# Attention decode: P times V summed in four PSUM quadrants instead of one row

## The chip, the cores and the metric

The kernel runs on one core of a Trainium2 chip. The metric is the device time of one execution in microseconds, the median over the runs. A profile of one execution is taken beside the times; its span runs from the first to the last instruction on the core, and some time of the execution lies outside of it.

## The reference

One query row for each of 16 heads attends to 8192 keys of width 256; everything is bfloat16.

```
B, H, Sq, Sk, D = 1, 16, 1, 8192, 256
scale = q.shape[-1] ** -0.5
scores = jnp.einsum("bhqd,bhkd->bhqk", q, k) * scale
p = softmax(scores, axis=-1)
return jnp.einsum("bhqk,bhkd->bhqd", p, v)
```

K and V are 67 MB each and every element is used once.

## The kernel before, in words

**Tiles.** A head's K (and V) is one SBUF buffer of 128 partitions by 64 x 256: partition p holds the keys 64p to 64p + 63, and "column j" means the 128 keys 64p + j, a block of 128 x 256. There are two K buffers and two V buffers, used by even and odd heads.

**Scores.** VectorE makes the scores of columns 0 to 47 (`head`, line 191: multiply a block by the query, which stands in every partition, and sum along the row). TensorE makes those of columns 48 to 63: it transposes the blocks (`ktrans`, line 280), ScalarE copies the transposes to SBUF (`evac`, line 376), and matmuls with the query give 16 columns of scores (`kscore`, line 294), which ScalarE copies (`scopy`, line 380) next to VectorE's.

**Softmax.** VectorE reduces the 64 scores of each partition to a maximum (line 207). A matmul lays these 128 maxima into one row of the PSUM tile `mx` (`transpose_m`, line 228, columns 0 to 127), VectorE takes their maximum (`xmax`, line 173), a matmul with ones spreads it over the partitions (`bcast`, line 234), and ScalarE computes the exponentials E and their sum per partition (`expo`, lines 384 and 388). A matmul with ones adds the sums (`total`, line 244), VectorE takes the reciprocal (`recips`, line 178).

**P times V.** `pv` (line 259) runs 64 matmuls: the stationary operand is one column of E (128 x 1), the moving one a block of V (128 x 256), and all 64 are summed in row 0 of the PSUM tile `acc` of the head's parity. ScalarE scales that row by the reciprocal (`final`, line 401) and issues the output's DMA (line 408).

**Order.** Each engine has its own queue, written out by hand; semaphores join them. A loop turn handles two heads. TensorE in turn i: scores of the even head 2i; `pv` of head 2i-2, with `transpose_m`, `bcast` and `total` of head 2i-1 placed behind its columns 32, 48 and 64; scores of the odd head 2i+1; `pv` of head 2i-1; `total` of head 2i. ScalarE in turn i: the four copies, `scopy` and the next query for each of the two heads, the exponentials where they come due, and at the end of the turn `final` of heads 2i-2 and 2i-1. VectorE: the even head, then the odd head; the reciprocals of the two heads before stand behind column 2 of each. After the loop the exponentials and the two finals of heads 14 and 15 follow.

**Loads.** SyncE issues all K and V loads in one order (line 136): K of head h+2, then V of head h. K of head h+2 waits until VectorE has finished head h (`kd`), V of head h until `pv` of head h-2 is done. A load is 4096 KB; the V of heads 14 and 15 comes in pieces, that of head 15 in nine, the last two of two columns each, so that `pv` can follow the data closely. The semaphores that stand for "the round before" are given their first values by GpSimd (`AHEAD`), behind its memsets at the start.

Of the kernel before, what the change touches and what calls it, by code (L numbers as in the profile page):

```python
# [6 lines left out]
ACT = mybir.ActivationFunctionType  # L7
AX = mybir.AxisListType
FP32 = mybir.dt.float32
# [4 lines left out]
K_FIRST = (16, 32)  # L14
V_HALVED = 13
V_LATE = {14: (0, 16, 32, 48), 15: (0, 16, 28, 38, 46, 52, 57, 60, 62)}
AHEAD = {"kd": 1, "sc": 1, "sp": 2, "ex": 2, "m": 1, "g": 1, "mT": 1, "l": 2, "bc": 1, "nb": 1, "rc": 2, "pv": 2, "fin": 4}
V_SEMS = (("va0", "v0b", "v0c", "v0d"), ("va1", "v1b", "v1c", "v1d", "v1e", "v1f", "v1g", "v1i", "v1j"))


class _Step:
# [19 lines left out]
def bass_standalone__mha_softmax__decode_kernel(nc: bass.Bass, q: bass.AP, k: bass.AP, v: bass.AP, out: bass.AP):  # L41
    B, H, Sq, D = q.shape
    Sk = k.shape[2]
    P = 128
    J = Sk // P
# [26 lines left out]
    with contextlib.ExitStack() as ctx:  # L72

        def sb(name, shape, d):
            return ctx.enter_context(nc.sbuf_tensor(name, shape, d))
# [19 lines left out]
        m = sb("m", [P, 2], FP32)  # L95
        g = sb("g", [1, 2], FP32)
# [4 lines left out]
        identb = sb("identb", [P, P], BF16)  # L101
        ones_row = sb("ones_row", [1, P], FP32)
        ones_col = sb("ones_col", [P, 1], FP32)
        o_sb = [sb(f"o_sb{i}", [1, D], out.dtype) for i in range(2)]

        acc = [ps(f"acc{i}", [P, 512]) for i in range(2)]
        tp = [ps(f"tp{i}", [P, GRP * D], BF16) for i in range(2)]
        spe = ps("spe", [P, 512])
        mx = ps("mx", [P, 512])
# [2 lines left out]

        for name in ("qc", "pool", "cb", "cf", "qp", "qs", "qb", "kd", "tp", "kt", "sp", "sc", "m", "mT", "g", "bc", "nb", "ex"):
            sem(name)
        for name in ("l", "rc", "pv", "fin", "ldq", "k0", "k0a", "k0b", "k1", "va0", "va1", "v1h", "o0", "o1"):
            sem(name)
        late = [name for row in V_SEMS for name in row[1:] if name not in ("v0c", "v1c")] + ["v1h"]
        for row in V_SEMS:
# [6 lines left out]
        if True:  # L125
# [15 lines left out]
            @(lambda f: f(nc.gpsimd))  # L141
            def _(pool):
                def step(ins, n):
                    ins.then_inc(sem("pool"), 1)
                    pool.wait_ge(sem("pool"), n)

                def eye(t, n, done):
                    step(pool.memset(t[:, :], 0.0), n)
                    pool.affine_select(
                        out=t[:, :],  # L150
                        in_=t[:, :],
                        compare_op=ALU.not_equal,
                        fill=1.0,
                        base=0,
                        pattern=[[-1, P]],
                        channel_multiplier=1,
                    ).then_inc(sem(done), 1)

                eye(identb, 1, "cb")
                eye(ident, 2, "cf")  # L160
                pool.memset(ones_row[:, :], 1.0).then_inc(sem("cf"), 1)
                pool.memset(ones_col[:, :], 1.0).then_inc(sem("cf"), 1)
                pool.memset(q_all[:, H * QW : (H + 1) * QW], 0.0).then_inc(sem("cf"), 1)
                for name, n in AHEAD.items():
                    pool.nop().then_inc(sem(name), n)
                for name in late + ["o0", "o1", "va0", "va1"]:
                    pool.nop().then_inc(sem(name), 32 if name in ("o0", "o1") else 16)
# [57 lines left out]
            def _(pe):  # L225
# [16 lines left out]
                def total(h):  # L242
# [6 lines left out]
                        stop=True,  # L249
                    ).then_inc(sem("l"), 1)  # L250

                def pv(h, waits, at):

                    pe.wait_ge(sem("fin"), h.of(1, 3))
                    pe.wait_ge(sem(f"va{h.par}"), h.of(8, 32 - 8 * h.par))
                    for j in range(J):
                        for name, value in waits.get(j, ()):
                            pe.wait_ge(sem(name), value)
                        ins = pe.matmul(  # L259
                            acc[h.par][0:1, 0:D],  # L260
                            lhsT=E[h.par][:, j : j + 1],
                            rhs=vbuf[h.par][:, j * D : (j + 1) * D],
                            start=(j == 0),
                            stop=(j == J - 1),
                        )
                        if j == J - 1:
                            ins.then_inc(sem("pv"), 1)
                        if j + 1 in at:
                            at[j + 1]()
# [33 lines left out]
                def scores(t, before=None):  # L303
# [15 lines left out]
                    rhs=q_sb[:, :],  # L319
# [26 lines left out]
                with pe.Fori(0, H // 2 + 1) as i:  # L346
                    ev, od = _Step(0, i), _Step(1, i)
                    fin_turn = pe.snap((i // 8) * 16 + 16)
                    half_turn = pe.snap(((i + 1) // 8) * 16 + 16)
                    old = od.back(2)  # L350
                    with pe.If(i < H // 2):
                        scores(ev)
                    with pe.If(i > 0):
                        pv(
                            ev.back(2),
                            {V_LATE[14][n]: [(V_SEMS[0][n], fin_turn)] for n in range(1, len(V_SEMS[0]))},
                            {32: lambda: transpose_m(old), 48: lambda: bcast(old), 64: lambda: total(old)},
                        )
                    with pe.If(i < H // 2):
                        scores(od, before=ev)  # L360
                    with pe.If(i > 0):
                        waits = {V_LATE[15][n]: [(V_SEMS[1][n], fin_turn)] for n in range(1, len(V_SEMS[1]))}
                        waits[HALF] = [("v1h", half_turn)]
                        pv(old, waits, {})
                    with pe.If(i < H // 2):
                        total(ev)

            @(lambda f: f(nc.scalar))
            def _(act):
# [12 lines left out]
                def expo(h):  # L382
                    act.wait_ge(sem("bc"), h.of(1, 2))
                    act.activation(  # L384
                        out=negb[:, h.par : h.par + 1], in_=sm[:, 0:1], func=ACT.Copy, scale=-1.0
                    ).then_inc(sem("nb"), 1)
                    act.wait_ge(sem("nb"), h.of(1, 2))
                    act.activation(  # L388
                        out=E[h.par][:, :],
                        in_=S[h.par][:, :],  # L390
                        func=ACT.Exp,
                        bias=negb[:, h.par : h.par + 1],
                        scale=1.0,
                        accum_out=lsum[:, h.par : h.par + 1],
                    ).then_inc(sem("ex"), 1)

                def final(h, dst):
                    act.wait_ge(sem("rc"), h.of(1, 3))
                    act.wait_ge(sem("pv"), h.of(1, 3))
                    act.wait_ge(sem(f"o{h.par}"), h.of(8, 32 - 8 * h.par))  # L400
                    act.activation(  # L401
                        out=o_sb[h.par][0:1, :],
                        in_=acc[h.par][0:1, 0:D],
                        func=ACT.Copy,
                        scale=recip[0:1, h.par : h.par + 1],
                    ).then_inc(sem("fin"), 1)
                    act.wait_ge(sem("fin"), h.of(1, 5))
                    act.dma_start(dst, o_sb[h.par][0:1, :]).then_inc(sem(f"o{h.par}"), 16)
# [24 lines left out]
                with act.Fori(0, H // 2) as i:  # L433
                    for c in (0, 1):
                        t = _Step(c, i)
                        for gi in range(NG):
                            evac(t, gi)
                        if c:
                            expo(t.back(1))
                        scopy(t)  # L440
                        act.wait_ge(sem("kd"), t.of(1, 1))
                        q_copy(_Step(c + 1, i), q_all[:, bass.ds(i * (2 * QW) + (c + 1) * QW, QW)])
                        with act.If(i > 0):
                            if c == 0:
                                expo(t.back(1))
                            else:
                                for d in (0, 1):
                                    at = nc.s_assert_within(
                                        (i - 1) * (2 * D) + d * D,
                                        0,  # L450
                                        (H - 1) * D,
                                        skip_runtime_bounds_check_because="the branch is taken from turn 1 on",
                                    )
                                    final(t.back(3 - d), flat[:, bass.ds(at, D)])
                expo(_Step(H - 1))
                for h in (H - 2, H - 1):
                    final(_Step(h), out[0, h, 0:1, :])
                for i in range(2):
# [30 lines left out]
```

## Time and profile before

| | before |
|---|---|
| time, median of 2 runs | 320.21 us (320.20 to 320.22) |
| span of the profiled execution | 318.6 us |
| granted TensorE clock, mean over the span | 0.839 |
| PE / VectorE / ScalarE busy | 69% / 86% / 29% |
| moved by DMA | 134.29 MB, mean 422 GB/s |

The profiled execution's own time is its span of 318.6 us and what lies around it; the timed runs are 1.6 us above the span.

In the rows of the profile, L259 is line 259 of the kernel, PE stands for TensorE's matmuls, PEld for its weight loads, DVE for VectorE, ACT for ScalarE, POOL for GpSimd, SPq and ACTq for DMA issues on the queues of SyncE and ScalarE. A row of the timeline has the start in us, the length, the engine and the operation, with the number of instructions merged into the row (x8), and in brackets the idle time ahead of it with what ended it. A row of a group has, behind a bar, the busy time in us and the mean duration in ns. A DMA row has the number of issues, the size of one and the median time from issue to landing. A row of a stretch has, for PE, PEld, DVE, ACT and POOL in this order, the busy time and the number of instructions, then the granted clock, the DMA engines' share and the GB/s. An fp32 matmul shows as two instructions.

### The profile page before, as it was taken

How to read it: one execution, taken by the hardware profiler on the slowest of the kernel's cores; microseconds unless marked ns; L12 is line 12 of the kernel's file. 1: busy time of each engine (PE TensorE's matmuls, PEld its weight loads, DVE VectorE, ACT ScalarE, POOL GpSimd, SP SyncE). 2: the span in 40 equal slices, each digit the busy share in tenths (PEclk: the TensorE clock that was granted, in tenths of full speed). 3: DMA queues.
4: the chain of work that ended last, by engine and by line, in shares of the span. 5: the costliest groups of instructions: out<-in, count | busy, mean ns of one | idle time of the engine just before them, and what ended most of it. 6: DMA issues, size and time to landing. Idle time of an engine off the chain costs nothing.

```text
span 318.6 us, 6833 instructions
## 1 busy us (share of the span) xinstructions
PE 219.2 (69%) x2163; PEld 156.0 (49%) x2163; DVE 275.2 (86%) x1584; ACT 92.5 (29%) x172; POOL 1.6 (0%) x11
## 2 busy tenths in 40 slices
PE   4446185988775947949387482975739668497987
PEld 1335163656553634727256262663626446266664
DVE  3989999999999898897988979799798897979920
ACT  5436050333215050330505114051330603306010
POOL 1000000000000000000000000000000000000000
PEclk9999999659797875957879597695977859699999
DMA  7999999999999999999999999999999999999995
GB/s 303 447 418 465 393 455 407 448 416 448 412 448 428 428 444 411 453 412 453 420 436 440 416 448 407 453 416 449 424 432 444 411 449 416 444 405 428 419 416 201
DMA packets 6981, 134.29 MB, mean 422 GB/s; under 512 B 800, under 2 KB 1216, under 8 KB 1856
## 3 DMA queue, kind: packets, MB, share of 16 engines
q1 hardware_dynamic: 6912, 134.22, 98.6%
q8 instruction: 2, 0.03, 0.0%
q10 hardware_dynamic: 64, 0.02, 0.0%
q14 instruction: 3, 0.02, 0.0%
HBM read 134.23 MB, written 0.01 MB: 421 GB/s over the span
## 4 chain that ended last, share of the span: by engine, by line
DMA 64%; PE 19%; DVE 15%; SPq 1%; issue 1%; ACT 0%; DVEq 0%; ACTq 0%
DMA vbuf<-in_v_dram 58%; PE acc L259 18%; DVE kbuf L191 14%; DMA kbuf<-in_k_dram 7%; SPq L136 1%; DVE S L191 0%; DVE g L173 0%; PE sm L234 0%; ACT o_sb L401 0%; DVE recip L178 0%; DVEq L209 0%; DVEq L183 0%; PE qps L244 0%; DVE m L207 0%; ACTq L400 0%
## 5 line engine op out<-in xcount | busy, mean ns | idle before, releaser
L191 DVE CUSTOM_DVE_ANT_0 kbuf<-kbuf,q_now 128x256 bf16<-128x256 bf16 x768 | 268.4, 409 | 21.3 <-DMA kbuf<-in_k_dram 20.4
L259 PE MATMUL acc<-vbuf,E 128*1 128x256 bf16 x1024 | 147.1, 313 | 41.6 <-DMA vbuf<-in_v_dram 41.4
L259 PEld LDWEIGHTS acc<-vbuf,E 128*1 128x1 bf16 x1024 | 95.5, 95 | 86.2 <-DMA vbuf<-in_v_dram 44.4
L376 ACT ACTIVATE KT<-tp 128x1024 bf16<-128x1024 bf16 x64 | 62.3, 1021 | 46.4 <-PE tp L280 45.9
L191 DVE DVE_READ_ACCUMULATOR2_ANT S<- 128x1 f32 x768 | 55.2, 72 | 0.0
L280 PE MATMUL tp<-identb,kbuf 128*128 128x128 bf16 x512 | 42.2, 239 | 14.7 <-DMA kbuf<-in_k_dram 14.5
L280 PEld LDWEIGHTS tp<-identb,kbuf 128*128 128x128 bf16 x512 | 33.6, 107 | 18.1 <-DMA kbuf<-in_k_dram 12.1
L294 PE MATMUL spe<-q_now,KT 128*128 128x1 bf16 x512 | 22.9, 166 | 27.3 <-ACT KT L376 27.0
L294 PEld LDWEIGHTS spe<-q_now,KT 128*128 128x128 bf16 x512 | 18.1, 99 | 35.7 <-ACT KT L376 26.1
L401 ACT ACTIVATE o_sb<-acc,recip 1x256 bf16<-1x256 f32 x16 | 7.3, 458 | 87.0 <-PE acc L259 85.7
L384 ACT ACTIVATE negb<-sm 128x1 f32<-128x1 f32 x16 | 2.8, 174 | 83.8 <-PE sm L234 83.8
L173 DVE TENSOR_REDUCE g<-mx 1x1 f32<-1x128 f32 x16 | 4.4, 276 | 7.5 <-PE mx L228 7.5
L234 PE MATMUL sm<-g,ones_row 1*128 1x1 f32 x32 | 6.5, 268 | 5.0 <-DVE g L173 5.0
L228 PE MATMUL mx<-ident,m 128*1 128x128 f32 x32 | 6.5, 287 | 4.3 <-DVE m L207 4.3
L234 PEld LDWEIGHTS sm<-g,ones_row 1*128 1x128 f32 x32 | 5.1, 198 | 7.1 <-DVE g L173 5.6
L371 ACT ACTIVATE q_now<-q_all 128x258 bf16 x16 | 6.7, 418 | 0.1
L178 DVE RECIPROCAL recip<-qps 1x1 f32<-1x1 f32 x16 | 2.4, 152 | 3.9 <-PE qps L244 3.9
L388 ACT ACTIVATE E<-S,negb 128x64 bf16<-128x64 f32 x16 | 5.6, 348 | 0.5
L336 PE MATMUL acc<-q_sb,identb 16*128 16x256 bf16 x16 | 4.3, 404 | 0.8 <-ACT q_all L426 0.8
L228 PEld LDWEIGHTS mx<-ident,m 128*1 128x1 f32 x32 | 2.1, 82 | 5.1 <-DVE m L207 4.8
L426 ACT ACTIVATE q_all<-acc 128x512 bf16<-128x512 f32 x8 | 4.3, 592 | 0.6 <-PE acc L336 0.6
L380 ACT ACTIVATE S<-spe 128x16 f32<-128x16 f32 x16 | 2.9, 184 | 3.6 <-PE spe L294 3.6
(24 smaller groups left out, 18.5 us busy)
## 6 DMA issues: line engine op xcount, KB each, us to landing
kbuf<-in_k_dram SPq DMA_DIRECT2D x15, 4096.0 KB, 20.3
vbuf<-in_v_dram SPq DMA_DIRECT2D x11, 4096.0 KB, 28.7
vbuf<-in_v_dram SPq DMA_DIRECT2D x6, 2048.0 KB, 24.4
vbuf<-in_v_dram SPq DMA_DIRECT2D x5, 1024.0 KB, 14.8
kbuf<-in_k_dram SPq DMA_DIRECT2D x2, 1024.0 KB, 5.8
kbuf<-in_k_dram SPq DMA_DIRECT2D x1, 2048.0 KB, 11.3
vbuf<-in_v_dram SPq DMA_DIRECT2D x1, 768.0 KB, 10.2
vbuf<-in_v_dram SPq DMA_DIRECT2D x1, 640.0 KB, 11.3
```

Of the source, the lines that this page charges most:

```text
L173: dve.tensor_reduce(g[0:1, h.par : h.par + 1], mx[0:1, 0:P], AX.X, ALU.max).then_inc(sem("g"), 1)
L191: ins = dve.tensor_tensor_reduce(out=buf[:, j * D : (j + 1) * D], in0=buf[:, j * D : (j + 1) * D], in1=q_now[h.par][:, 0:D], scale=SCALE, ...
L228: pe.matmul(mx[0:1, 0:P], lhsT=m[:, h.par : h.par + 1], rhs=ident[:, :], start=True, stop=True).then_inc(sem("mT"), 1)
L234: pe.matmul(sm[:, 0:1], lhsT=ones_row[0:1, 0:P], rhs=g[0:1, h.par : h.par + 1], start=True, stop=True,).then_inc(sem("bc"), 1)
L259: ins = pe.matmul(acc[h.par][0:1, 0:D], lhsT=E[h.par][:, j : j + 1], rhs=vbuf[h.par][:, j * D : (j + 1) * D], start=(j == 0), stop=(j == J ...
L280: ins = pe.transpose(tp[gi % 2][:, b * D + hf * P : b * D + (hf + 1) * P], buf[:, j * D + hf * P : j * D + (hf + 1) * P], identb[:, :],)
L294: ins = pe.matmul(spe[:, c : c + 1], lhsT=KT[gi % 2][:, b * D + hf * P : b * D + (hf + 1) * P], rhs=q_now[h.par][:, D + hf : D + hf + 1], ...
L336: ins = pe.matmul(acc[pair % 2][:, (h % 2) * D : (h % 2 + 1) * D], lhsT=identb[0:H, h : h + 1].to_broadcast([H, P]), rhs=q_sb[:, :], start ...
L371: act.activation(out=q_now[h.par][:, :], in_=src_q, func=ACT.Copy).then_inc(sem("qb"), 1)
L376: act.activation(out=KT[gi % 2][:, :], in_=tp[gi % 2][:, :], func=ACT.Copy).then_inc(sem("kt"), 1)
L388: act.activation(out=E[h.par][:, :], in_=S[h.par][:, :], func=ACT.Exp, bias=negb[:, h.par : h.par + 1], scale=1.0, accum_out=lsum[:, h.par ...
L401: act.activation(out=o_sb[h.par][0:1, :], in_=acc[h.par][0:1, 0:D], func=ACT.Copy, scale=recip[0:1, h.par : h.par + 1],).then_inc(sem("fin ...
```

## The change

Column j of V is summed in the PSUM row of quadrant j mod 4, that is in rows 0, 32, 64 and 96 of `acc`. When a head's 64 matmuls are done, ScalarE copies rows 0 to 96 of `acc` into an SBUF tile `comb` (`collect`); a matmul whose stationary operand `sel` is one at the four rows and zero elsewhere adds them into row 0 of `mx`, columns 256 to 511 (`gather`); ScalarE scales that row as before (`final`). The gathers of both heads of a turn stand on TensorE behind the `pv` of the odd head, and the collects of both heads stand on ScalarE in front of the two finals. A gather waits until the final of the head before it has read the row.

```
+TILE = 32
+ROWS = 3 * TILE + 1
...
+        comb = [sb(f"comb{i}", [ROWS, D], FP32) for i in range(2)]
+        sel = sb("sel", [ROWS, 1], FP32)
...
+                step(pool.memset(sel[:, :], 0.0), 3)
+                for n, r in enumerate(range(0, ROWS, TILE)):
+                    step(pool.memset(sel[r : r + 1, :], 1.0), n + 4)
...
+                def gather(h):
+                    pe.wait_ge(sem("cm"), h.of(1, 3))
+                    pe.wait_ge(sem("fin"), h.of(1, 4))
+                    pe.matmul(
+                        mx[0:1, D : 2 * D], lhsT=sel[:, :], rhs=comb[h.par][:, :], start=True, stop=True
+                    ).then_inc(sem("sl"), 1)
...
-                    pe.wait_ge(sem("fin"), h.of(1, 3))
+                    pe.wait_ge(sem("fin"), h.of(1, 4 - h.par))
...
                         ins = pe.matmul(
-                            acc[h.par][0:1, 0:D],
+                            acc[h.par][j % 4 * TILE : j % 4 * TILE + 1, 0:D],
...
-                            start=(j == 0),
-                            stop=(j == J - 1),
+                            start=(j < 4),
+                            stop=(j >= J - 4),
...
                         pv(old, waits, {})
+                        gather(ev.back(2))
+                        gather(old)
...
+                def collect(h):
+                    act.wait_ge(sem("pv"), h.of(1, 3))
+                    act.activation(out=comb[h.par][:, :], in_=acc[h.par][0:ROWS, 0:D], func=ACT.Copy).then_inc(sem("cm"), 1)
...
                 def final(h, dst):
                     act.wait_ge(sem("rc"), h.of(1, 3))
-                    act.wait_ge(sem("pv"), h.of(1, 3))
+                    act.wait_ge(sem("sl"), h.of(1, 3))
...
-                        in_=acc[h.par][0:1, 0:D],
+                        in_=mx[0:1, D : 2 * D],
...
                                 for d in (0, 1):
+                                    collect(t.back(3 - d))
+                                for d in (0, 1):
...
                 expo(_Step(H - 1))
+                for h in (H - 2, H - 1):
+                    collect(_Step(h))
```

More of the change, by code (lines that the diff above doesn't have):

```diff
@@ L16 @@
 V_LATE = {14: (0, 16, 32, 48), 15: (0, 16, 28, 38, 46, 52, 57, 60, 62)}
-AHEAD = {"kd": 1, "sc": 1, "sp": 2, "ex": 2, "m": 1, "g": 1, "mT": 1, "l": 2, "bc": 1, "nb": 1, "rc": 2, "pv": 2, "fin": 4}
+AHEAD = {"kd": 1, "sc": 1, "sp": 2, "ex": 2, "m": 1, "g": 1, "mT": 1, "l": 2, "bc": 1, "nb": 1, "rc": 2, "pv": 2, "fin": 4, "cm": 2, "sl": 2}
 V_SEMS = (("va0", "v0b", "v0c", "v0d"), ("va1", "v1b", "v1c", "v1d", "v1e", "v1f", "v1g", "v1i", "v1j"))
+TILE = 32
+ROWS = 3 * TILE + 1
 class _Step:
@@ L114, in bass_standalone__mha_softmax__decode_kernel @@
             sem(name)
-        for name in ("l", "rc", "pv", "fin", "ldq", "k0", "k0a", "k0b", "k1", "va0", "va1", "v1h", "o0", "o1"):
+        for name in ("l", "rc", "cm", "sl", "pv", "fin", "ldq", "k0", "k0a", "k0b", "k1", "va0", "va1", "v1h", "o0", "o1"):
             sem(name)
```

## The prediction

> **What bounds the kernel now.** I read the page's header, its slices and its queues first, to see whether any resource is full; then the chain of waits; then the timeline and the stretches of the last microseconds.
>
> ```profile
> span 318.6 us, 6833 instructions
> ...
> PEclk9999999659797875957879597695977859699999
> DMA  7999999999999999999999999999999999999995
> ...
> q1 hardware_dynamic: 6912, 134.22, 98.6%
> ...
> DMA 64%; PE 19%; DVE 15%; SPq 1%; issue 1%; ACT 0%; DVEq 0%; ACTq 0%
> ...
> kbuf<-in_k_dram SPq DMA_DIRECT2D x15, 4096.0 KB, 20.3
> vbuf<-in_v_dram SPq DMA_DIRECT2D x11, 4096.0 KB, 28.7
> ```
>
> The reader is to see one full resource. The queue that carries K and V keeps the 16 DMA engines busy for 98.6% of the span, in every slice but the first and the last. It moves 134.22 MB, so 134.22 / 318.6 = 0.421 MB per us; a load of 4096 KB (4.19 MB) needs 10.0 us of the engines, and a pair of heads (four loads) 39.8 us. But a K load lands 20.3 us after its issue and a V load 28.7 us after: work for 10.3 us and 18.7 us is still ahead of it in the queue when it is issued. Whoever issues such a load some microseconds later or earlier changes the depth of the queue and not the rate. The chain of waits puts 19% on PE, but its pieces run from a V landing over 64 matmuls to the issue of a later V load that then queues for 28.7 us. Shorter PE pieces in this chain become longer DMA pieces. So only what lies behind the last landing counts.
>
> These are the last microseconds, from the timeline, the DMA issues and the stretches.
>
> ```profile
> 303.32 0.91 SPq L136 DMA_DIRECT2D vbuf<-in_v_dram  x2
> ...
> vbuf<-in_v_dram SPq DMA_DIRECT2D x2, 128.0 KB, 12.7
> ...
> L259 PEld LDWEIGHTS acc<-vbuf,E x1024: 79/84/128, 44.8 to 316.5; 128*1 128x1 bf16 x171
> L259 PE MATMUL acc<-vbuf,E x1024: 269/273/421, 44.8 to 316.6; 128*1 128x256 bf16 x171
> ...
> 314.63 0.52 PEld L259 LDWEIGHTS acc<-vbuf,E 128*1 128x1 bf16 x6 [0.27 <-DMA vbuf<-in_v_dram]
> 315.41 1.18 PEld L259 LDWEIGHTS acc<-vbuf,E 128*1 128x1 bf16 x12 [0.26 <-DMA vbuf<-in_v_dram]
> 316.97 0.47 ACT L401 ACTIVATE o_sb<-acc,recip 1x256 bf16<-1x256 f32 x1 [8.15 <-PE acc L259]
> 317.47 0.24 ACTq L408 DMA_DIRECT2D out_dram<-o_sb  x1
> ...
> 316.00:317.00 1.00, 0.89 (x9) 0.39 (x6) 0.00 (x0) 0.03 (x1) 0.00 (x0) 1.00 0.00 0
> ```
>
> Two issues take 0.91 us from 303.32, so the last, the 128 KB of columns 62 and 63, starts near 303.8 and lands near 303.8 + 12.7 = 316.5. The last matmul starts at 316.6. PE is thus not behind the data: it has caught up at column 46 (314.63) and again at column 52 (315.41), where its weight loads wait for the DMA. The last 12 weight loads take 1.18 us, 0.1 us apart, which brings column 62 to about 316.5, just when it lands; the DMA engines move nothing from 316 on (share 0.00), and PE still has its full clock (1.00). Behind that come ScalarE's final at 316.97 and the output's DMA, whose end closes the span at 318.6, 1.6 us after the final began. The measured median is 320.21, so 1.6 us lie outside the span.
>
> **The change part by part.**
>
> *The 64 matmuls of a head.* None is removed. Each now goes to one of four PSUM quadrants. No row shows two matmuls of different quadrants side by side. From above, the pace stays at today's 0.1 us; from below, the nearest rows are the score matmuls:
>
> ```profile
> L294 PE MATMUL spe<-q_now,KT 128*128 128x1 bf16 x512 | 22.9, 166 | 27.3 <-ACT KT L376 27.0
> ...
> 288.37 0.35 PE L294 MATMUL spe<-q_now,KT 128*128 128x1 bf16 x8 [0.67 <-ACT KT L376]
> ...
> 293.00:295.00 2.00, 2.00 (x21) 1.55 (x19) 2.00 (x13) 0.00 (x0) 0.00 (x0) 1.00 0.91 385
> ```
>
> Eight of them with one moving column end within 0.35 us, that is (0.35 - 0.17) / 7 = 0.026 us apart (0.17 is their mean duration), against 2.00 us / 21 = 0.095 us in a stretch full of P times V. I expect something between, nearer the lower end, since the streams can overlap. A head then takes 64 x 0.026 = 1.7 us to 6.1 us at full clock where the data is there. The gain at the end is nearly nothing: after the landing at 316.5 two matmuls are left, and one of them can start 0.07 to 0.1 us earlier. I take 0, since the landing decides.
>
> *What is added at the end of a turn.* Until now ScalarE read row 0 of each head. Now it copies 97 x 256 of each head (collect), PE multiplies by the ones (gather, fp32, one bank slot for both heads), ScalarE scales (final), and the second gather waits for the first final. The rows to price it:
>
> ```profile
> L414 ACT ACTIVATE q_now<-spe 128x256 bf16<-128x256 f32 x1 | 0.4, 384 | 1.7 <-PE qps L324 1.7
> L401 ACT ACTIVATE o_sb<-acc,recip 1x256 bf16<-1x256 f32 x16 | 7.3, 458 | 87.0 <-PE acc L259 85.7
> ...
> 308.00 0.19 PEld L244 LDWEIGHTS qps<-ones_col,lsum 128*1 128x1 f32 x2
> 308.11 0.19 PE L244 MATMUL qps<-ones_col,lsum 128*1 128x1 f32 x2
> ...
> 303.99 0.38 PE L228 MATMUL mx<-ident,m 128*1 128x128 f32 x2 [0.38 <-DVE m L207]
> ...
> 59.45 0.23 PE L244 MATMUL qps<-ones_col,lsum 128*1 128x1 f32 x2
> 59.55 0.59 PE L228 MATMUL mx<-ident,m 128*1 128x128 f32 x2
> ```
>
> Collect: a 128 x 256 copy out of PSUM took 0.384 us and a 1 x 256 one 0.458, so rows are free; I take 0.40. Gather: an fp32 matmul shows as two passes. With 1 moving column they take 0.19 us, with 128 columns 0.38, so 128 more columns cost another 0.19: 0.57 for 256, and the weight load leads by 0.11 (308.00 to 308.11): 0.68. From below (columns free) 0.30; from above the slow-clock pair at 59.5, where 0.23 becomes 0.59: 0.59 + 0.36 + 0.11 = 1.06. I take 0.68, as the last stretch runs at clock 1.00.
>
> *The sum at the end.* The last matmul ends and ScalarE starts at 316.97, as before, but with collect of head 15, to 317.37. Gather of head 14 needs nothing of that; it is issued behind the last matmul (316.6) and ends near 317.3. Final of head 14: 317.41 to 317.88 (0.04 for a semaphore, 0.47). Gather of head 15: 317.92 to 318.60. Final of head 15 starts at 318.64 instead of 316.97: 1.67 us later. The remaining 1.6 us are as before: span 320.2, time 320.21 + 1.67 = **321.9**. Head 14, whose final ran ahead of these matmuls, now stands in this chain too, because its gather is queued behind head 15's matmuls.
>
> *The same chain in the middle.* At the end of each turn PE and ScalarE now go through gather, final, gather: 0.68 + 0.04 + 0.47 + 0.04 + 0.68 = 1.9 us, and behind it on PE stand total and the next scores, on ScalarE the next evacuations. The first who needs one of these is VectorE, whose reciprocal waits for total:
>
> ```profile
> 267.11 0.19 PE L244 MATMUL qps<-ones_col,lsum 128*1 128x1 f32 x2
> 267.17 0.43 DVE L191 CUSTOM_DVE_ANT_0 kbuf<-kbuf,q_now 128x256 bf16<-128x256 bf16 x1 [2.10 <-DMA kbuf<-in_k_dram]
> 268.21 0.15 DVE L178 RECIPROCAL recip<-qps 1x1 f32<-1x1 f32 x1
> 273.08 0.18 ACT L380 ACTIVATE S<-spe 128x16 f32<-128x16 f32 x1 [0.45 <-PE spe L294]
> 285.04 0.22 DVE L207 TENSOR_REDUCE m<-S 128x1 f32<-128x64 f32 x1
> ```
>
> Total would end near 267.30 + 1.9 = 269.2, 1.0 us behind the reciprocal's slot at 268.21. VectorE would stall for 1.0 us per turn, unless faster matmuls end the turn earlier. The copy of PE's scores, which VectorE needs just ahead of its last reduction at 285.04, moves from 273.08 to 275: no wait. VectorE idles 2.10 us for K ahead of that head anyway, and a K issue that comes 1.0 us late finds 10.3 us of queued work. I cost it at nothing; without that cover it would be 8 turns x 1.0 = 8 us.
>
> *Preparation.* GpSimd gets five small memsets, each waiting for the one before, in front of the increments that release the engines.
>
> ```profile
> 0.73 0.20 POOL L148 MEMSET identb<- 128x128 bf16 x1 [0.29 <-POOLq L474]
> 1.17 0.29 POOL L149 TENSOR_SCALAR_AFFINE_SELECT identb<-identb 128x128 bf16<-128x128 bf16 x1 [0.23 <-POOL identb L148]
> 2.16 0.30 POOL L163 MEMSET q_all<- 128x258 bf16 x1
> 5.54 0.42 DVE L191 CUSTOM_DVE_ANT_0 kbuf<-kbuf,q_now 128x256 bf16<-128x256 bf16 x1 [5.54 <-DMA kbuf<-in_k_dram]
> ```
>
> At 0.20 + 0.23 us each they add 2.2 us: GpSimd's last memset ends at 4.7 instead of 2.46. VectorE starts at 5.54, released by K's landing. Cost nothing. If the increments took over 0.8 us more, VectorE would start later by the excess, under the same cover of queued loads.
>
> **The rivals.**
>
> *The clock falls in the last stretch.* If the quadrants overlap, PE is less busy, and these rows show what idleness does:
>
> ```profile
> 271.00:273.00 2.00, 1.16 (x26) 0.85 (x22) 2.00 (x13) 1.63 (x2) 0.00 (x0) 1.00 0.95 410
> 275.00:277.00 2.00, 0.10 (x1) 0.09 (x2) 2.00 (x13) 0.00 (x0) 0.00 (x0) 0.50 0.84 360
> 279.00:281.00 2.00, 2.00 (x15) 1.39 (x14) 2.00 (x13) 0.00 (x0) 0.00 (x0) 0.75 1.07 459
> ```
>
> A PE that does next to nothing is granted 0.50, one busy for 1.16 of 2 us keeps 1.00. With gathers of 1.06 us head 14's gather ends at 317.66, its final at 318.17, the second gather at 319.27, and the final starts at 319.31: +2.3, 322.5. Against it: the pieces of V keep PE at work, those at 314.63 and 315.41 only 0.8 us apart, so no idle stretch should last for 2 us. The Trainium skill ("TensorE: Matmul & The Clock Gate", Part 1) says that the clock halves after an idle window of about 3.4 us and returns after a busy one; the trace agrees in size, 0.50 after the idle stretch and still 0.75 at 279 to 281, when PE is full again. By that rule the clock holds. Chance 0.2.
>
> *Quadrant changes stop the pipeline (slower).* If each matmul had to drain before one of another quadrant loads, it would cost 0.084 + 0.273 = 0.36 us (the medians of the two rows of L259 above) instead of 0.1. A turn's PE work would be 128 x 0.36 = 46 us, plus 2 x 6.0 us of scores (from total at 267.11 to the copy at 273.08) and the 1.9 us of the new chain, against 39.8 us of DMA: 60 - 39.8 = 20 us more in each of 8 turns, 480 us. It decides from (39.8 - 13.9) / 128 = 0.20 us per matmul. For it: nothing in the trace; against it: the weight loads follow each other under running matmuls today, 0.1 us apart. The Trainium skill ("TensorEngine Tiling (Array Packing)", Key Properties) says that a change of the tiling mode drains the engine, a change of tile alone does not; no row here shows either, and by it only the step from these matmuls to a gather would drain, one matmul of 0.27 us: 322.1. Chance 0.03.
>
> *The 1.9 us of each turn are not covered.* 8 x 1.9 = 15 us, 335. It needs an empty DMA queue at a K issue; 98.6% speaks against. Chance 0.04.
>
> *The chain of waits is right as it stands.* Its 19% on PE, 60 us, would shrink to a third: 320 - 40 = 280. Same objection; chance 0.02.
>
> *The loads end differently.* A queue filled otherwise could end 1 to 2 us earlier or later, which hides or doubles the 1.67. The two runs before lie 0.02 apart, which speaks for a fixed end. Chance 0.11.
>
> **How the numbers follow.** The forecast (+1.67) has 0.60: 321.9, and 321.5 if the second gather costs its lower bound of 0.30 (the first hides behind the collect then). The slow clock takes the range to 322.5. An end of the loads that shifts by up to 0.7 us, which I take for half of the last rival, widens it on either side: 320.8 to 323.2. That leaves out 0.03 + 0.04 + 0.02 and half of 0.11, 0.15 in all. A change of 2% (6.4 us) is what a measurement of this kernel surely tells from none; only the three large rivals pass it: faster 0.02, slower 0.07, same 0.91.
>
> **What would show it.** Right: the span grows by 1 to 2.5 us and all of it behind the last V landing near 316.5; two collects of 0.4, gathers as two fp32 passes of 0.6 to 0.7 us together, and the final of head 15 near 318.6; DMA share near 98%; idle time of PE waiting for V goes up by what P times V loses. Wrong: matmuls of L259's kind at 0.2 us or more apart, zeros in the DMA slices ahead of the end, a last landing more than a microsecond away from 316.5, or VectorE's waits for total far above 1 us per turn.

## The result and the profile after

The changed kernel takes 322.75 us (322.67 to 322.84, 2 runs) against 320.21 us (320.20 to 320.22, 2 runs): a ratio of 1.008, with an interval of 1.0051 to 1.0110. That is 2.54 us more, inside the stated range of 320.8 to 323.2 and 0.85 us above the 321.9 of the forecast. The span of the profiled execution is 321.3 us, 2.7 more than before.

From the page of the changed kernel:

```profile
span 321.3 us, 6944 instructions
...
PEclk9999999995665755557555555756655575555575
DMA  7999999999999999999999999999999999999991
...
q1 hardware_dynamic: 6912, 134.22, 97.7%
...
DMA 53%; DVE 41%; issue 2%; PE 2%; SPq 1%; ACT 0%; DVEq 0%; ACTq 0%
...
L275 PE MATMUL acc<-vbuf,E 128*1 128x256 bf16 x1024 | 62.9, 407 | 43.8 <-DMA vbuf<-in_v_dram 43.1
...
L296 PE MATMUL tp<-identb,kbuf 128*128 128x128 bf16 x512 | 62.8, 310 | 42.9 <-DMA kbuf<-in_k_dram 42.9
...
kbuf<-in_k_dram SPq DMA_DIRECT2D x15, 4096.0 KB, 21.7
vbuf<-in_v_dram SPq DMA_DIRECT2D x11, 4096.0 KB, 31.1
```

The groups of the same matmuls and of the same transposes in the page of the kernel before:

```profile
L259 PE MATMUL acc<-vbuf,E 128*1 128x256 bf16 x1024 | 147.1, 313 | 41.6 <-DMA vbuf<-in_v_dram 41.4
...
L280 PE MATMUL tp<-identb,kbuf 128*128 128x128 bf16 x512 | 42.2, 239 | 14.7 <-DMA kbuf<-in_k_dram 14.5
```

The loads are as full as before: nines in all slices between the first and the last, 97.7% of a longer span. P times V (now line 275) keeps PE busy for 62.9 us instead of 147.1, and not one microsecond of that shows in the time. The chain of waits has lost its PE share, 19% to 2%, and VectorE has gained in it, 15% to 41%, while the DMA's share fell from 64% to 53%. Each load lies longer in the queue, 21.7 and 31.1 us instead of 20.3 and 28.7, and V is issued earlier: the first half of head 13's, for example, at 265.54 instead of 267.31. The other difference is the granted clock, which is 5 in most slices where the kernel before mostly had 7 to 9; its mean over the span is 0.651 against 0.839.

The last microseconds, from the timeline and the stretches of the changed kernel:

```profile
309.15 1.02 PE L275 MATMUL acc<-vbuf,E 128*1 128x256 bf16 x16 [1.86 <-DMA vbuf<-in_v_dram]
...
315.65 1.53 PE L275 MATMUL acc<-vbuf,E 128*1 128x256 bf16 x12 [0.19 <-DMA vbuf<-in_v_dram]
...
316.81 0.08 PEld L275 LDWEIGHTS acc<-vbuf,E 128*1 128x1 bf16 x2 [0.24 <-DMA vbuf<-in_v_dram]
316.99 0.11 PEld L264 LDWEIGHTS mx<-comb,sel 97*1 97x1 f32 x2
317.02 1.01 PE L264 MATMUL mx<-comb,sel 97*1 97x256 f32 x2
317.23 0.39 ACT L417 ACTIVATE comb<-acc 97x256 f32<-97x256 f32 x1 [9.52 <-PE acc L275]
318.11 0.47 ACT L423 ACTIVATE o_sb<-mx,recip 1x256 bf16<-1x256 f32 x1 [0.50 <-PE mx L264]
...
318.63 1.01 PE L264 MATMUL mx<-comb,sel 97*1 97x256 f32 x2 [0.60 <-ACT o_sb L423]
319.73 0.47 ACT L423 ACTIVATE o_sb<-mx,recip 1x256 bf16<-1x256 f32 x1 [1.15 <-PE mx L264]
...
316.00:317.00 1.00, 1.00 (x12) 0.27 (x8) 0.00 (x0) 0.00 (x0) 0.00 (x0) 0.50 0.02 7
```

Columns 62 and 63 still wait for their data (weight loads at 316.81, released by the DMA). Behind that stands the chain as forecast: collect of head 15 beside the gather of head 14, final of head 14, gather of head 15, final of head 15 at 319.73 instead of 316.97. But each gather lasts 1.01 us, and the clock of the stretch is 0.50. A smaller part of the difference lies ahead of the chain: collect starts at 317.23, 0.26 us behind the place of the old final, since the last columns came later in this execution (316.81; 316.55 in experiment 2, 316.63 in experiment 3).

### The profile page after: what moved, and what is told of

Read it like the earlier page. It is cut to its first block, busy times and chain, and to the rows that moved or that the text cites. A ratio compares the mean times of both kernels' runs of the same rounds, so it can differ in the third digit from the quotient of the medians.

```text
span 321.3 us, 6944 instructions
## 1 busy us (share of the span) xinstructions
PE 172.2 (54%) x2195; PEld 115.4 (36%) x2195; DVE 274.7 (85%) x1584; ACT 100.2 (31%) x188; POOL 2.0 (1%) x16
## 3 DMA queue, kind: packets, MB, share of 16 engines
q1 hardware_dynamic: 6912, 134.22, 97.7%
## 4 chain that ended last, share of the span: by engine, by line
DMA 53%; DVE 41%; issue 2%; PE 2%; SPq 1%; ACT 0%; DVEq 0%; ACTq 0%
DMA kbuf<-in_k_dram 39%; DVE kbuf L200 39%; DMA vbuf<-in_v_dram 14%; DVE S L200 2%; SPq L142 1%; PE acc L275 1%; PE mx L264 1%; DVE g L182 1%; ACT o_sb L423 0%; DVE recip L187 0%; DVEq L192 0%; DVEq L218 0%; DVE m L216 0%; ACTq L422 0%; DVEq L191 0%
## 5 line engine op out<-in xcount | busy, mean ns | idle before, releaser
L200 DVE CUSTOM_DVE_ANT_0 kbuf<-kbuf,q_now 128x256 bf16<-128x256 bf16 x768 | 268.4, 409 | 29.6 <-DMA kbuf<-in_k_dram 28.6
L275 PE MATMUL acc<-vbuf,E 128*1 128x256 bf16 x1024 | 62.9, 407 | 43.8 <-DMA vbuf<-in_v_dram 43.1
L296 PE MATMUL tp<-identb,kbuf 128*128 128x128 bf16 x512 | 62.8, 310 | 42.9 <-DMA kbuf<-in_k_dram 42.9
L296 PEld LDWEIGHTS tp<-identb,kbuf 128*128 128x128 bf16 x512 | 50.7, 143 | 48.0 <-DMA kbuf<-in_k_dram 43.1
L275 PEld LDWEIGHTS acc<-vbuf,E 128*1 128x1 bf16 x1024 | 31.9, 114 | 63.6 <-DMA vbuf<-in_v_dram 48.1
L310 PEld LDWEIGHTS spe<-q_now,KT 128*128 128x128 bf16 x512 | 20.7, 109 | 26.4 <-ACT KT L394 21.6
L417 ACT ACTIVATE comb<-acc 97x256 f32<-97x256 f32 x16 | 6.0, 376 | 45.5 <-PE acc L275 45.5
L264 PE MATMUL mx<-comb,sel 97*1 97x256 f32 x32 | 13.5, 515 | 6.1 <-ACT o_sb L423 6.1
L237 PE MATMUL mx<-ident,m 128*1 128x128 f32 x32 | 9.7, 406 | 12.1 <-DVE m L216 12.1
L423 ACT ACTIVATE o_sb<-mx,recip 1x256 bf16<-1x256 f32 x16 | 7.4, 465 | 11.5 <-PE mx L264 11.5
L264 PEld LDWEIGHTS mx<-comb,sel 97*1 97x1 f32 x32 | 2.5, 98 | 13.7 <-ACT o_sb L423 12.6
## 6 DMA issues: line engine op xcount, KB each, us to landing
kbuf<-in_k_dram SPq DMA_DIRECT2D x15, 4096.0 KB, 21.7
vbuf<-in_v_dram SPq DMA_DIRECT2D x11, 4096.0 KB, 31.1
```

The lines of the kernel that those rows point to most:

```text
L200: ins = dve.tensor_tensor_reduce(out=buf[:, j * D : (j + 1) * D], in0=buf[:, j * D : (j + 1) * D], in1=q_now[h.par][:, 0:D], scale=SCALE, ...
L237: pe.matmul(mx[0:1, 0:P], lhsT=m[:, h.par : h.par + 1], rhs=ident[:, :], start=True, stop=True).then_inc(sem("mT"), 1)
L264: pe.matmul(mx[0:1, D : 2 * D], lhsT=sel[:, :], rhs=comb[h.par][:, :], start=True, stop=True).then_inc(sem("sl"), 1)
L275: ins = pe.matmul(acc[h.par][j % 4 * TILE : j % 4 * TILE + 1, 0:D], lhsT=E[h.par][:, j : j + 1], rhs=vbuf[h.par][:, j * D : (j + 1) * D], ...
L296: ins = pe.transpose(tp[gi % 2][:, b * D + hf * P : b * D + (hf + 1) * P], buf[:, j * D + hf * P : j * D + (hf + 1) * P], identb[:, :],)
L310: ins = pe.matmul(spe[:, c : c + 1], lhsT=KT[gi % 2][:, b * D + hf * P : b * D + (hf + 1) * P], rhs=q_now[h.par][:, D + hf : D + hf + 1], ...
```

## The experiments

Each is timed in five rounds beside the kernel before on the same chip: 320.23 us for the first four, 320.12 for the others.

**1. One row, with the new chain.** Quadrants undone, everything else kept.

```
-                            acc[h.par][j % 4 * TILE : j % 4 * TILE + 1, 0:D],
+                            acc[h.par][0:1, 0:D],
...
-                            start=(j < 4),
-                            stop=(j >= J - 4),
+                            start=(j == 0),
+                            stop=(j == J - 1),
...
-                    step(pool.memset(sel[r : r + 1, :], 1.0), n + 4)
+                    step(pool.memset(sel[0:1, :], 1.0), n + 4)
```

> All 64 matmuls of a head are summed in row 0 again, and sel is one at row 0 alone; collect, gather and final stay as in the change. My theory: of the 2.54 us that the change costs, the new chain at the end costs 1.67 at full clock, and the rest, some 0.85, comes from the clock of 0.50 at which the two gathers then run, because PE with four quadrants is too idle. With one row PE stays busy and at clock 1.00 in the last 10 us as before, a gather takes 0.6 to 0.7 us, the time is 321.9 and the span 320.2. Rival: the fp32 gather takes 1.0 us whatever PE did before it, or the loads end later for another reason: then 322.6 to 322.8 here too.

Measured: 323.39 us (323.01 to 323.75), ratio 1.0096 (1.0080 to 1.0111). Neither theory said that. The timeline and two stretches of this run's profiled execution, which is the slowest of its four (323.75):

```profile
301.42 0.60 PE L264 MATMUL mx<-comb,sel 97*1 97x256 f32 x2
...
304.09 3.65 PE L275 MATMUL acc<-vbuf,E 128*1 128x256 bf16 x32 [0.65 <-ACT o_sb L423]
...
311.72 6.87 PEld L275 LDWEIGHTS acc<-vbuf,E 128*1 128x1 bf16 x64
...
318.92 0.38 ACT L417 ACTIVATE comb<-acc 97x256 f32<-97x256 f32 x1 [6.65 <-PE acc L275]
...
293.00:295.00 2.00, 2.00 (x10) 1.20 (x11) 2.00 (x13) 0.79 (x4) 0.00 (x0) 0.50 0.98 414
...
312.00:316.00 4.00, 4.00 (x40) 3.07 (x38) 0.08 (x1) 0.27 (x1) 0.00 (x0) 1.00 0.70 258
```

The gathers are at 0.60 and the clock in the last microseconds is 1.00, as my theory had it. But the 64 weight loads of head 15 run without a break from 311.72, where the kernel before waited for a piece of V again and again: PE is behind the data and reaches the end 1.9 us late (collect at 318.92; the final stood there at 316.97 before). The rows at the top show how it fell behind. P times V of head 14 starts at 304.09, having waited 0.65 us for the final of head 13, which closes the chain of the turn before; in the timeline of the kernel before it started at 299.96:

```profile
299.96 3.65 PE L259 MATMUL acc<-vbuf,E 128*1 128x256 bf16 x32
```

So the chain costs a second time, in the last turn but one: 2.67 of these 4.13 us lie between its first gather (301.42) and 304.09. The rest stood ahead of the chain: P times V of head 13 began at 292.96 instead of 291.99, and at a clock of 0.50 (the stretch from 293 to 295), where the kernel before had 1.00. One row per head leaves PE no room to make any of it up.

**2. Quadrants alone.** The kernel before with the matmuls spread and nothing else; final reads row 0, so three quarters of the sum are left out.

```
-                            acc[h.par][0:1, 0:D],
+                            acc[h.par][j % 4 * 32 : j % 4 * 32 + 1, 0:D],
...
-                            start=(j == 0),
-                            stop=(j == J - 1),
+                            start=(j < 4),
+                            stop=(j >= J - 4),
```

> The kernel before with the matmuls spread over the four quadrants and nothing else: no collect, no gather, and final reads row 0 alone, so three quarters of the sum over the keys are left out. My theory: the quadrants by themselves gain or lose nothing, since the last landing decides: 320.2, within 0.3, last landing near 316.5 to 316.8, clock near 0.5 in the last 10 us. Rival A: the chain of waits with 19% on PE is the bound, and the time falls far below 320. Rival B: the quadrants shift the loads themselves by 0.3 us or more (the last piece landed at about 316.8 in the changed kernel against 316.5): 320.5 to 320.8.

Measured: 320.19 us, ratio 1.0000 (0.9991 to 1.0009). The timeline and a stretch:

```profile
316.55 0.08 PEld L259 LDWEIGHTS acc<-vbuf,E 128*1 128x1 bf16 x2 [0.24 <-DMA vbuf<-in_v_dram]
317.02 0.46 ACT L401 ACTIVATE o_sb<-acc,recip 1x256 bf16<-1x256 f32 x1 [9.03 <-PE acc L259]
...
312.00:316.00 4.00, 2.60 (x32) 0.61 (x32) 0.00 (x0) 0.00 (x0) 0.00 (x0) 0.50 0.67 246
```

The matmuls at a fraction of the time are worth nothing by themselves; the last columns are loaded at 316.55, as before, and the final starts at 317.02 against 316.97. Rivals A and B fall. The slow clock is there too (0.50), so it comes with the quadrants, not with the chain.

**3. Early gather.** The even head's gather moves ahead of the odd head's matmuls.

```
+                        gather(ev.back(2))
                         pv(old, waits, {})
-                        gather(ev.back(2))
                         gather(old)
...
                                 for d in (0, 1):
                                     collect(t.back(3 - d))
-                                for d in (0, 1):
...
                 for h in (H - 2, H - 1):
                     collect(_Step(h))
-                for h in (H - 2, H - 1):
```

> The changed kernel with the gather of the even head placed on PE ahead of the P times V of the odd head, and on ScalarE collect and final of a head next to each other. At the end only collect, gather and final of head 15 are left in a row. In the changed kernel's timeline the final of head 15 starts at 319.73, the collect of head 15 at 317.23; here the gather can start at 317.66 and takes 1.05 at the slow clock, so the final starts at 318.75: 0.98 us earlier, 321.8. Rival: the serial chain of both heads is not what costs, and the time stays at 322.7.

Measured: 321.70 us (321.65 to 321.75), ratio 1.0047 (1.0033 to 1.0060), against 321.8 expected. The timeline shows the short chain:

```profile
317.05 0.39 ACT L417 ACTIVATE comb<-acc 97x256 f32<-97x256 f32 x1 [7.41 <-PE acc L275]
...
317.57 1.01 PE L264 MATMUL mx<-comb,sel 97*1 97x256 f32 x2 [0.56 <-ACT comb L417]
318.67 0.47 ACT L423 ACTIVATE o_sb<-mx,recip 1x256 bf16<-1x256 f32 x1 [1.23 <-PE mx L264]
```

1.05 of the change's 2.54 us is thus the place of head 14's gather and final.

**4. Fillers.** Matmuls that nobody needs behind the pieces of an odd head's V.

```
+                def fill(h, j, n):
+                    for _ in range(n):
+                        pe.matmul(
+                            acc[h.par][0:1, D : 2 * D],
+                            lhsT=E[h.par][:, j : j + 1],
+                            rhs=vbuf[h.par][:, j * D : (j + 1) * D],
+                            start=False,
+                            stop=False,
+                        )
...
-                        pv(old, waits, {})
+                        ends = V_LATE[15][1:7]
+                        pv(old, waits, {b: (lambda a=a, b=b: fill(old, a, (b - a) // 2)) for a, b in zip(V_LATE[15], ends)})
```

> The changed kernel with idle work for PE behind each piece of an odd head's V but the last three: half as many matmuls as the piece has columns, all to quadrant 0, into columns of the PSUM tile that nobody reads. Theory of the clock: PE now runs one stream through the last 10 us and is granted 1.00 there instead of 0.50; each gather falls from 1.0 to 0.6 us, the time by some 0.8 to 321.9. Rival: the clock is not what makes the gathers slow, or fillers delay the real matmuls behind the landings: 322.7 or more.

Measured: 321.81 us (321.77 to 322.01), ratio 1.0050 (1.0037 to 1.0064). From the timeline and the stretches:

```profile
316.99 0.59 PE L264 MATMUL mx<-comb,sel 97*1 97x256 f32 x2
...
318.86 0.47 ACT L434 ACTIVATE o_sb<-mx,recip 1x256 bf16<-1x256 f32 x1 [0.73 <-PE mx L264]
...
312.00:316.00 4.00, 4.00 (x46) 2.53 (x44) 0.00 (x0) 0.00 (x0) 0.00 (x0) 0.63 0.68 250
316.00:318.00 2.00, 1.58 (x20) 0.72 (x14) 0.00 (x0) 0.72 (x2) 0.00 (x0) 1.00 0.01 5
```

Work that only keeps PE active makes the kernel 0.94 us faster: the clock is 1.00 at the end, the gathers fall from 1.01 to 0.59, and the last final starts at 318.86 instead of 319.73. That the slow clock is what made the gathers slow is thereby shown. The clock was not 1.00 through the last 10 us, as I had expected: it was 0.63 from 312 to 316 and 1.00 from 316 on, in time for the gathers.

**5. Odd heads in one row.** Four quadrants for the even heads only; the chain as in the change.

```
+                def row(h, j):
+                    return 0 if h.par else j % 4 * TILE
...
-                            acc[h.par][j % 4 * TILE : j % 4 * TILE + 1, 0:D],
+                            acc[h.par][row(h, j) : row(h, j) + 1, 0:D],
...
-                        mx[0:1, D : 2 * D], lhsT=sel[:, :], rhs=comb[h.par][:, :], start=True, stop=True
+                        mx[0:1, D : 2 * D], lhsT=sel[:, h.par : h.par + 1], rhs=comb[h.par][:, :], start=True, stop=True
```

> The changed kernel with four quadrants for the even heads alone; the odd heads are summed in row 0 (their stationary column of ones is one at row 0 alone); the chain at the end of a turn is as in the change. With one row for all heads it took 323.4 and PE worked through the last 14 us without a gap, behind the data, because P times V of head 14 has to wait for the final of head 13, the end of the new chain of the turn before. Theory: that backlog is what the quadrants repay, and head 14 alone repays it; head 15 in one row then follows the data at 0.11 us per column against 0.155 of the loads, keeps the clock at 1.00, and the gathers take 0.6: 321.8, as with the fillers. Rival: one row in the last head costs by itself: 323.0 or more.

Measured: 321.96 us, ratio 1.0062 (1.0048 to 1.0076), 1.3 to 1.4 us less than with one row for all heads in experiment 1 (1.84 us above the kernel before on the same chip, against 3.16). The timeline and a stretch:

```profile
304.62 1.16 PE L278 MATMUL acc<-vbuf,E 128*1 128x256 bf16 x32 [0.70 <-ACT o_sb L426]
...
308.92 1.61 PEld L278 LDWEIGHTS acc<-vbuf,E 128*1 128x1 bf16 x16 [1.46 <-DMA vbuf<-in_v_dram]
...
316.56 0.09 PEld L278 LDWEIGHTS acc<-vbuf,E 128*1 128x1 bf16 x2 [0.20 <-DMA vbuf<-in_v_dram]
...
318.66 0.47 ACT L426 ACTIVATE o_sb<-mx,recip 1x256 bf16<-1x256 f32 x1 [0.73 <-PE mx L264]
...
312.00:316.00 4.00, 3.87 (x33) 2.19 (x31) 0.00 (x0) 0.00 (x0) 0.00 (x0) 1.00 0.67 247
```

P times V of head 14 starts even later than in experiment 1 (304.62 against 304.09), but its first 32 matmuls take 1.16 us instead of 3.65, and head 15 in one row waits for its data again, from its first piece (308.92) to its last (316.56), at full clock. So the excess of experiment 1 is the backlog of head 14.

**6. Two quadrants.** Column j goes to row 0 or 32.

```
-                            acc[h.par][j % 4 * TILE : j % 4 * TILE + 1, 0:D],
+                            acc[h.par][j % 2 * TILE : j % 2 * TILE + 1, 0:D],
...
-                            start=(j < 4),
-                            stop=(j >= J - 4),
+                            start=(j < 2),
+                            stop=(j >= J - 2),
...
-                    step(pool.memset(sel[r : r + 1, :], 1.0), n + 4)
+                    step(pool.memset(sel[r % 64 : r % 64 + 1, :], 1.0), n + 4)
```

> The changed kernel with two quadrants (column j to row 0 or 32). If the streams of different quadrants run side by side, the pace at the slow clock is 0.107 us per matmul (0.213 with one row, 0.053 with four), and 64 matmuls take 6.8 us there. The clock: with twice the time per head PE is busier; theory says the grant follows the time in which at least one stream runs, so the mean over the span lies between the 0.65 of four quadrants and the 0.84 to 0.86 of one row, and the time at 322 to 322.8, by the clock it has at the end. Rival: the pace does not depend on the number of quadrants (no overlap, but a shorter drain): 0.05 here as well.

Measured: 321.91 us (321.70 to 322.69), ratio 1.0061 (1.0047 to 1.0075); the mean clock is 0.728, between the two as expected, and the time is 0.1 us under the 322 to 322.8 that I had expected. Rows of the timeline of this run, of the changed kernel and of the kernel before:

```profile
277.08 3.57 PE L275 MATMUL acc<-vbuf,E 128*1 128x256 bf16 x32 [4.10 <-DMA vbuf<-in_v_dram]
...
300.99 1.91 PE L275 MATMUL acc<-vbuf,E 128*1 128x256 bf16 x32 [0.66 <-ACT o_sb L423]
```

```profile
141.21 3.58 PE L275 MATMUL acc<-vbuf,E 128*1 128x256 bf16 x64 [3.15 <-DMA vbuf<-in_v_dram]
```

```profile
56.09 3.57 PE L259 MATMUL acc<-vbuf,E 128*1 128x256 bf16 x16
```

At the slow clock 3.57 us hold 32 matmuls with two quadrants, 64 with four, and 16 with one. Sixteen rounds take (3.57 - 0.42) / 15 = 0.21 us each (0.42 is the longest matmul of the kernel before), whether a round is one, two or four matmuls: a pace of 0.21, 0.105 and 0.053 us. One stream for each quadrant runs beside the others in full, and the rival falls. At the full clock the 32 of the second row take (1.91 - 0.27) / 15 = 0.11 us a round, the pace of one row before. PE had its full clock in the last 2 us here, and the time is that of the fillers.

**7. Early gather in bfloat16.** Experiment 3 with one more change.

```
-        comb = [sb(f"comb{i}", [ROWS, D], FP32) for i in range(2)]
-        sel = sb("sel", [ROWS, 1], FP32)
+        comb = [sb(f"comb{i}", [ROWS, D], BF16) for i in range(2)]
+        sel = sb("sel", [ROWS, 1], BF16)
```

> The early gather (321.70) with the collected rows and the ones in bfloat16, so that the four partial sums are rounded once more, and the gather is one pass. Two fp32 passes took 1.01 at the slow clock, one bf16 pass of 256 columns takes 0.42: 0.6 less in the chain, 321.1. Rival: the gather's time is the wait around it and not the passes: 321.5 or more.

Measured: 321.14 us (median of 6), ratio 1.0031 (1.0019 to 1.0043). The line of the gathers and the last one in the timeline:

```profile
L264 PE MATMUL mx<-comb,sel x16: 269/372/373, 67.4 to 318.4; 97*1 97x256 bf16 x16
...
318.40 0.37 PE L264 MATMUL mx<-comb,sel 97*1 97x256 bf16 x1 [0.55 <-ACT comb L417]
318.86 0.47 ACT L423 ACTIVATE o_sb<-mx,recip 1x256 bf16<-1x256 f32 x1 [0.59 <-PE mx L264]
```

One pass of 0.37 in place of 1.01 is worth about 0.5 us: 0.56 from median to median, 0.45 when each is taken from the kernel before on its own chip (1.02 and 1.47 us above it). (This profile's last V piece landed late, at about 317.5, so its starts are not to be set beside those of the other runs.)

**8. Odd heads without the gather.** Early gather; odd heads in one row, read by final directly, as before the change; even heads as in the change.

```
+                    if h.par:
+                        pe.nop().then_inc(sem("sl"), 1)
+                        return
                     pe.matmul(
                         mx[0:1, D : 2 * D], ...
...
+                    if h.par:
+                        act.nop().then_inc(sem("cm"), 1)
+                        return
                     act.activation(out=comb[h.par][:, :], ...
...
-                        in_=mx[0:1, D : 2 * D],
+                        in_=(acc[1][0:1, 0:D] if h.par else mx[0:1, D : 2 * D]),
```

> Early gather; even heads in four quadrants with collect and gather, odd heads in row 0 with the final reading it directly, as before the change. Head 15 thus has no gather, and the eight gathers of the even heads lie beside loads. Theory (only what stands behind the last landing counts): 320.2, the time of the kernel before, within 0.3. Rival: gathers in the middle of the kernel cost something too, 0.2 us or more each, 1.5 us in all.

Measured: 320.39 us (median of 11), ratio 1.0015 (1.0000 to 1.0030), 0.27 us above the kernel before: the theory's 0.3 holds, and eight collects and gathers beside loads cost together no more than that. Whether the 0.27 is real the interval leaves open. No version with quadrants that was run beats the kernel before. Experiment 2, without collect and gather, stands at 320.19: while the last landing sets the end, I expect nothing below that.

## Why the prediction was right, and where it was off

**The bound** was right. Quadrants alone changed the time by nothing (experiment 2), the depth of the queue took up what PE gave back, and the rival that read the chain of waits as it stands is out. The trap is in that view: 64% on DMA and 19% on PE is a chain of things that released each other, not of things that would make it shorter. Two details of my reading did not come true. The PE pieces of that chain did not become DMA pieces: VectorE's share rose instead, 15% to 41%. And I had named as a sign that PE's wait for V would grow by what P times V loses. P times V lost 84 us, and PE's wait for V grew by 1.7 (41.4 to 43.1). The rest went elsewhere: into the wait of PE's transposes for K (14.5 to 42.9), into the transposes themselves at the slower clock (42.2 to 62.8), and into smaller waits.

**The price of the new chain** was right in its structure and in all terms but one. Collect took 0.39 (0.40 taken), final 0.47 (0.47). The gather was the mis-sized term: I took 0.68 from weight load to end at full clock, and it took from 316.99 to 318.03 (317.02 + 1.01), or 1.04. The upper end that I had worked out from the slow pair at 59.5 us was 1.06, and the rival that used it gave 322.5, 0.25 from the measured 322.75. At full clock the forecast holds: 321.81 with fillers, 321.96 with the odd heads in one row, 321.91 with two quadrants, against 321.9 (1.58, 1.84 and 1.79 us above the kernel before on the same chip, against 1.67). The stated range held because it took in the slow clock: the forecast with 0.7 us for the end of the loads reaches only to 322.6.

**The choice between those clocks** was the step that failed: 0.60 for the forecast, 0.2 for the slow clock. I argued that pieces of V leave no idle stretch as long as 2 us and that PE at 1.16 us of 2 kept its clock. The idle gaps were indeed under 2 us (1.86 at 309.15, the longest behind 302), and the clock fell all the same, to 0.50 at 308.6, and stayed there. The trace of the kernel before already spoke against my argument. These stretches follow the one that I quoted:

```profile
273.00:273.20 0.20, 0.04 (x2) 0.00 (x0) 0.20 (x3) 0.12 (x1) 0.00 (x0) 0.94 0.76 328
273.20:273.40 0.20, 0.00 (x0) 0.00 (x0) 0.20 (x1) 0.18 (x2) 0.00 (x0) 0.50 1.52 655
```

PE's last matmul there ends at 273.04 (272.69 + 0.35), and the clock falls within 0.2 us of it. It did not wait for an idle stretch. The row that I quoted thus showed the clock that a run of one-row matmuls had left behind (1.00, with PE busy throughout, from 265 to 267), and not a clock that 1.16 us of work in 2 us would keep. Experiment 1 has such a fall too, at 292.6, with no gap of more than 0.67 us in the 7 us ahead of it. With four quadrants PE is active for a shorter time still; that this is why the clock fell fits experiments 2, 4 and 6, but how activity is measured is not shown. The Trainium skill's rule ("TensorE: Matmul & The Clock Gate", Part 1) of one idle window of about 3.4 us was not enough to exclude the fall: no such gap lies behind 302 in the changed kernel, so the measurement decides against reading the rule as "gaps below 3.4 us are safe".

**"I cost it at nothing" for the middle** held for the changed kernel, by the exception that I had named: the faster matmuls end the turn earlier. VectorE's reciprocal waits for total once, in the last head, where it waited twice before and waits five times with the chain and one row (experiment 1). The rows are of the changed kernel, the kernel before and experiment 1 (total, times, longest):

```profile
DVE recip L187 <- PE qps L253: 2.2, 1, 2.2
```

```profile
DVE recip L178 <- PE qps L244: 3.9, 2, 3.7
```

```profile
DVE recip L187 <- PE qps L253: 5.6, 5, 3.7
```

VectorE's waits for K did grow, from 20.4 to 28.6 us in all. They cost nothing here: experiment 2 has 28.3 and the time of the kernel before.

What I missed is another wait. In the last turn no scores lie between the turn's end and P times V of the even head, so that head waits for the final of head 13 (0.65 us in the changed kernel, at 301.93), and the start of the last 128 matmuls slips. By the code this wait is stricter than it has to be: the `acc` of head 14 was last read by the collect of head 12, for which the gather has already waited. No run here leaves it out. Experiment 1 shows the price without quadrants, 323.39, and experiment 5 that quick matmuls for the even heads alone take 1.3 to 1.4 us of it back. So the quadrants are worth something only inside this change: they repay part of the chain that they need.

**The rivals** of drained quadrants (0.20 us per matmul or more) and of an uncovered 1.9 us per turn are out, by a pace of 0.053 us and by the changed kernel's last microseconds, which hold all of the 2.5 us (the last final starts at 319.73 instead of 316.97). Nor does a drain show ahead of the gather: it starts at 317.02, and the last matmul of P times V ends at 317.18 (315.65 + 1.53), just ahead of the collect that waits for it (317.23).

## What to carry to other kernels

Ask first what is late after the gain: where loads fill the span and the last landing sets the end, four times the matmul rate bought nothing, and the steps that were added behind that landing (collect, gather, a second head's gather and final in front of it) set the price. Put what can be done earlier ahead of the last wait: moving one gather gave 1.05 us. And when an edit makes TensorE faster, price the operations behind it at the slow clock as well, since the clock can fall when the work becomes shorter (0.839 to 0.651 here).

## What the runs showed of the hardware that I had not expected

The clock fell when the work became shorter: its mean over the span is 0.839 with one row, 0.728 with two quadrants and 0.651 with four. Busy time alone does not say which clock is granted. These are stretches of the changed kernel:

```profile
287.00:289.00 2.00, 1.83 (x16) 1.56 (x16) 1.94 (x11) 0.98 (x2) 0.00 (x0) 0.50 0.98 418
289.00:291.00 2.00, 1.91 (x27) 1.88 (x27) 2.00 (x13) 0.97 (x3) 0.00 (x0) 0.50 1.00 426
...
301.79:305.20 3.41, 2.77 (x49) 1.60 (x50) 2.85 (x17) 0.01 (x1) 0.00 (x0) 0.50 1.01 423
305.20:308.61 3.41, 1.27 (x26) 0.79 (x21) 0.17 (x2) 1.00 (x4) 0.00 (x0) 1.00 1.01 417
308.61:312.02 3.41, 1.83 (x28) 0.61 (x28) 0.00 (x0) 0.00 (x0) 0.00 (x0) 0.50 1.01 405
```

PE is busy for 3.74 of 4 us between 287 and 291, with transposes and score matmuls, and stays at 0.50. It rises to 1.00 behind the 2.77 us from 301.79 on, which are nearly all P times V of head 14, and falls again behind the 1.27 us from 305.20 on. That transposes count for less than matmuls fits these rows, but no run here tests it.

The times of these changes have a pattern. The clock rises at 305.2 and falls at 308.6 in the changed kernel, 3.4 us apart; it falls at 292.6 and rises at 296.0 in experiment 1, 3.4 apart; and in the kernel before it falls at 273.2 and rises at 280.0, 6.8 apart. So in these traces the grant seems to be renewed in steps of 3.4 us, by the work of the step that ends, and a gap need not be as long as a step to lose it. How much work keeps it stays open.

The second surprise is how exactly the quadrants overlap: sixteen rounds of one, two or four matmuls with a 128 x 256 moving block took 3.57, 3.57 and 3.58 us.
